# Position-bias products of two chunks put two steps away from the attention's scores, and the left half of the bias tile read backwards from PSUM

## Chip, core and metric

The kernel runs on one core of a Trainium2 chip. The metric is device time in microseconds (us) of one execution. Five engines matter: TensorE (PE in the profile; PEld is its weight load), VectorE (DVE), ScalarE (ACT), GpSimd (POOL) and SyncE (SP). The last two issue most of the DMAs.

## What is computed

The reference runs attention with a position bias, then two feed-forward layers, on 4 batches, 8 heads, 576 positions and 64 features a head:

```python
scores = scale * np.matmul(q, k.transpose(0, 1, 3, 2))
x = (psi_rel / psi_i)[..., None]      # log1p|i-j| / log1p(max(i,1))
bias = np.maximum(x @ w1 + b1, 0.0) @ w2   # hidden 32, one value per head
attn = softmax(scores + bias) ;  attn_out = attn @ v
x = (sigmoid(x @ w_gate) * (x @ w_val)) @ w_out      # 512 -> 1536 -> 512
h = x @ w_in ;  out = (h * clip(h + 3, 0, 6) / 6) @ w_out2   # 512 -> 2048 -> 512
```

## The kernel before, in words

The 576 query positions are cut into five chunks (`QC`: 128, 128, 128, 128 and 64 rows, numbered 0 to 4). The attention of chunk 0 runs alone in a **lead**. Then come five **blocks**: block k runs the two feed-forward layers for the tokens of chunk k, 68 **steps** of twelve matmuls each (`product`, L554; kinds G and V, then Y, H and O, H, O), and between its steps stands the attention of chunk k+1. `block_events` makes a list of events, each with a due time counted in steps, and `block` runs an event ahead of the first step whose number is not below its due time. TensorE's order is just this order of writing. Beginning with block 1, the orders of ScalarE, VectorE and the DMA queues are chosen by a scheduler when the kernel is built; in block 0 it chooses ScalarE's and VectorE's.

The **bias of a chunk** is made one chunk ahead, in groups G of 16 rows. `bias_hidden` writes the hidden layer into tiles z (two calls on ScalarE, L147, two on VectorE, L149; two buffers). `bias_mm` multiplies by w2 (L160 in chunks 1 to 3, L168 in chunks 0 and 4). Chunks 1 to 3 are **mirrored**: only distances 0, 1, 2, ... are computed, once for each row, and `bias_out2` spreads two groups over a tile bo with rows of SU = 607 values: distances to the right in order, by ScalarE (L182), distances to the left in reverse order, by VectorE (L185). Two DMAs (L192) take bo to memory, from where `bias_read` fetches it as bm. `chunk_bias(c, t0, dt)` makes the events: z of group g at t0 + dt g, the products of groups g and g+1 at t0 + dt g + dt + 1.

The **attention of chunks 2 to 4** goes in pairs of (head pair, batch) units. For pair p `pair_qk` forms the scores (L426 in chunks 2 and 3): first the last 256 columns of both units, into two tiles of the pool `ps_m`, then the first 320 columns, one unit after the other, into two tiles of the pool `ps_s`. VectorE adds the bias and takes the minimum (L448), ScalarE takes exponentials (L314), VectorE normalises (L327) and transposes (L353), DMAs turn the result, and `pair_av` (L384) multiplies by the values, two pairs later.

The pool `ps_s` has two buffers in PSUM, taken in turn, and serves both the bias products and the 320-column scores:

```python
s1 = pool("ps_s", 2, space=PS)
m1 = pool("ps_m", 4, space=PS)
```

In block 1 the pairs stand at due times 21 + d i with d = (67 - 21)/9 = 5.11, and the products of chunk 3's bias at 31.21, 36.32, 41.43 and 46.54, each 0.01 of a step ahead of a pair. So TensorE meets, ahead of one step: `pair_av` of an old pair, the bias products, `pair_qk`. In block 2 d is 8.14, and the two products of chunk 4's bias come ahead of the pairs due at 16.79 and 33.07 in the same way.

Of the kernel before, what the change touches and what calls it, by code (L numbers as in the profile page):

```python
# [9 lines left out]
F32 = mybir.dt.float32  # L10
F32R = mybir.dt.float32r
U32 = mybir.dt.uint32
AF = mybir.ActivationFunctionType
ALU = mybir.AluOpType
AX = mybir.AxisListType

B, H, S, D = 4, 8, 576, 64
# [13 lines left out]
SU = S + 31  # L31
# [27 lines left out]
def fused_kernel(ctx: ExitStack, tc: tile.TileContext, qd, kd, vd, tz, td, rd, zc, w2b, iden, wpack, out):  # L59
    nc = tc.nc  # L60
# [21 lines left out]
    def mm_ps():  # L82
        return m1.tile([128, 512], F32, name="ps")
# [11 lines left out]
    cv_t = const.tile([128, 1], F32, name="cv_t")  # L95
# [11 lines left out]
    ps = mm_ps()  # L107
# [6 lines left out]
    ps = mm_ps()  # L114
    for g in (2, 3):
        nc.tensor.matmul(
            out=ps[32 * g:32 * g + 32, 0:2], lhsT=w2b_t, rhs=zc_t[:, 0:2], start=True, stop=True,
# [7 lines left out]
    A, z_q, bo_q = {}, {}, {}  # L125

    def mirrored(G):
        return QC[1][0] <= 16 * G < QC[NC - 1][0]

    def reach(G):  # L130

        i0 = 16 * (G & ~1)
        left, right = i0 + 31, S - 1 - i0
        return left, right, max(left, right) + 1

    def bias_hidden(G, g):

        if g == 0:
            z_q[G] = z_p.tile([128, 4, S], F32, name="z")
        t = 4 * G + g  # L140
        if mirrored(G):
            n = reach(G)[2]
            z, x = z_q[G][:, g, 0:n], td_t[:, 0:n]
        else:
            z, x = z_q[G][:, g], tz_t[:, S - 4 - 4 * t:2 * S - 4 - 4 * t]
        if g < 2:
            nc.scalar.activation(out=z, in_=x, func=AF.Relu, scale=sc_t[:, t:t + 1], bias=b1c)  # L147
        else:
            nc.vector.tensor_scalar(  # L149
                out=z, in0=x, scalar1=sc_t[:, t:t + 1], scalar2=zc_t[:, 2:3], op0=ALU.mult, op1=ALU.max  # L150
            )

    def bias_mm(G):
        z = z_q.pop(G)
        if mirrored(G):
            if G % 2 == 0:
                bo_q[G] = s_ps()
            ps, n = bo_q[G & ~1], reach(G)[2]
            for g in range(4):
                nc.tensor.matmul(  # L160
                    out=ps[32 * g:32 * g + 32, G % 2, 0:n], lhsT=w2b_t, rhs=z[:, g, 0:n],
                    start=True, stop=True, tile_position=(0, 32 * g),
                )
            return
        ps = bo_q[G] = s_ps()
        for j in range(2):
            for g in range(4):
                nc.tensor.matmul(  # L168
                    out=ps[32 * g:32 * g + 32, j, 0:NI], lhsT=w2b_t, rhs=z[:, g, NI * j:NI * j + NI],
                    start=True, stop=True, tile_position=(0, 32 * g),  # L170
                )

    bo_t = {}

    def bias_out2(G):

        ps = bo_q.pop(G)
        c = 16 * G // NQ
        i0 = 16 * G - QC[c][0]
        left, right, _ = reach(G)  # L180
        bo = A["bo"].tile([128, 2, SU], F32, name="bo")
        nc.scalar.activation(  # L182
            out=bo[:, :, left:], in_=ps[:, :, 0:right + 1], func=AF.Identity, scale=D ** 0.5, bias=cv_t
        )
        nc.vector.tensor_scalar(  # L185
            out=bo[:, :, left - 1::-1], in0=ps[:, :, 1:left + 1],
            scalar1=D ** 0.5, scalar2=cv_t, op0=ALU.mult, op1=ALU.add,
        )
        at = NQ - 32 - i0
        rows = biasD[c].rearrange("(h r w) -> r h w", h=H, w=SW)[i0:i0 + 32, :, at:at + SU]  # L190
        for x in range(2):
            nc.sync.dma_start(  # L192
                out=rows[16 * x:16 * x + 16], in_=bo[:, x],
            )

    def bias_out(G, x=0, last=True):

        ps = bo_q.pop(G)
        c = min(G // 8, NC - 1)
        if x == 0:  # L200
            bo_t[0] = A["bo"].tile([128, 2, SU], F32, name="bo")[:, :, 0:S]
        bo = bo_t[0][:, x]
        bv = bo.rearrange("p (a j) -> p a j", a=2)
        if c:
            nc.scalar.activation(out=bv, in_=ps[:, :, 0:NI], func=AF.Identity, scale=D ** 0.5, bias=cv_t)
        else:
            nc.vector.tensor_scalar(
                out=bv, in0=ps[:, :, 0:NI], scalar1=D ** 0.5, scalar2=cv_t, op0=ALU.mult, op1=ALU.add
            )
        i0 = 16 * G - QC[c][0]  # L210
        if c == 0:
            for h in range(2):
                nc.sync.dma_start(out=bm_q[0, 0][i0:i0 + 16, h], in_=bo.rearrange("(i h) j -> h i j", h=H)[h])
        if last:
            (nc.gpsimd if c == 0 else nc.sync).dma_start(
                out=biasD[c][i0 - 16 * x:i0 + 16].rearrange("(g i) h j -> (i h) g j", i=16),
                in_=bo_t[0][:, 0:x + 1],
            )
# [406 lines left out]
    with ExitStack() as lead:  # L625
# [11 lines left out]
        for G in range(NG0 + NG1 + 1):  # L637
            if G == NG0:
                bias_out(G - 1, (G - 1) % 2, G % 2 == 0)
            if G < NG0 + NG1:  # L640
                for g in range(4):
                    bias_hidden(G, g)
                bias_mm(G)
            if G and G < NG0:
                bias_out(G - 1, (G - 1) % 2, G % 2 == 0)
            if G == NG0 + NG1:
                bias_out2(NG0)
# [45 lines left out]
    def chunk_bias(c, t0, dt, done=0):  # L693

        i0, n = QC[c]
        G0, nG = i0 // 16 + done, n // 16 - done
        ev = []
        for g in range(nG):
            ev.append((t0 + dt * g, lambda G=G0 + g: [bias_hidden(G, t) for t in range(4)]))
        for g in range(0, nG, 2):  # L700
            def outs(G=G0 + g, two=min(2, nG - g)):
                for i in range(two):
                    bias_mm(G + i)
                if mirrored(G):
                    bias_out2(G)
                    return
                for i in range(two):
                    bias_out(G + i, i, i == two - 1)
            ev.append((t0 + dt * g + dt + 1, outs))
        return ev  # L710

    def chunk_att(c, t0, t1, lag):

        us = units[c]
        d = (t1 - t0) / (len(us) - 1 + lag)
        ev = [
            (t0 - 2 * d, lambda: att_load(us[0], False)),
            (t0 - d, lambda: (bias_read(us[0]), load_rows(us[1]), load_k(us[1]))),
        ]
        for i, u in enumerate(us):  # L720
            a = t0 + d * i

            def first(u=u, nxt=us[i + 2] if i + 2 < len(us) else None):
                if nxt:
                    load_rows(nxt)
                    load_k(nxt)
                att_qk(u)
                att_min(u)
                att_exp(u)
                att_norm(u)  # L730
            if i:
                ev.append((a + 0.5, lambda u=u: load_v(u)))
            for part in range(3):
                ev.append((a + lag * d - 3 + part, lambda u=u, p=part: att_tr(u, p, mm_ps)))
            ev.append((a + lag * d - 0.01, lambda u=u: (att_av(u, mm_ps), att_x(u))))
            ev.append((a, first))
        return ev
# [45 lines left out]
    def block_events(k):  # L783
        ev = []
        last = NSTEP - 1
        if k == 0:
            ev.append((1.0, lambda: nc.sync.dma_start(out=td_t[:, t0:], in_=td[:, t0:])))
            ev += chunk_bias(1, 2.0, 1.5, NG1)
            ev += chunk_att(1, 15.5, last, 2)
        elif k == 1:  # L790
            d = (last - 21.0) / 9
            ev += chunk_bias(2, 2.0, 1.5)
            ev += chunk_pairs(2, 21.0, d, 2 * d, last)
            ev += chunk_bias(3, 19.99 + 1.5 * d, d / 2)
        elif k == 2:
            d = (last - 9.5 - 0.5) / 7
            n4 = 2 * S - 4 - 4 * 16 * 8
            ev.append((0.1, lambda: nc.sync.dma_start(out=tz_t[:, 0:n4], in_=tz[:, 0:n4])))
            ev += chunk_pairs(3, 0.5, d, d, last)
            ev += chunk_bias(4, d - 0.51, d)  # L800
        elif k == 3:
            ev += chunk_pairs(4, 0.5, (last - 10.5) / 3, 10.0, last)
        return [e[::2] for e in sorted((e[0], n, e[1]) for n, e in enumerate(ev))]
# [90 lines left out]
```

## Time and profile before

| | |
|---|---|
| Time of the kernel before, median of 3 runs | 1126.38 us (1126.29 to 1127.05) |
| The profiled execution: its own time | 1126.06 us |
| The profiled execution: span of its instructions | 1124.3 us |
| TensorE busy | 1099.5 us, 98% of the span |
| VectorE, ScalarE, GpSimd busy | 670.3, 525.5, 126.1 us |

The span runs from the first to the last instruction; the execution's own time has 1.76 us more around it. Busy time is not the same as progress: an engine's share is an average over stages, and what a wait costs is read from the stage in which it stands.

### The profile page before, as it was taken

To read this page: it belongs to the slowest core of one execution; us is meant where nothing else is said; L and a number is where in the kernel's file an instruction comes from. 1 tells how busy PE (TensorE), PEld (TensorE's weight loads), DVE (VectorE), ACT (ScalarE), POOL (GpSimd) and SP (SyncE) were. 2 spreads that over 40 slices of the span, in tenths; PEclk is the share of its full clock that TensorE was granted. 3 is DMA by queue.
4 is the path that set the end of the run, shared out by engine and by line. 5 is a ranking of instruction groups with operands and counts; after the bars stand their busy time and mean duration, and the time that the engine had idled before them with its cause. 6 is when DMAs were issued, how large, how long until landed. Compare 5 with 4: busy or idle time off the path is not lost.

```text
span 1124.3 us, 19865 instructions
## 1 busy us (share of the span) xinstructions
PE 1099.5 (98%) x7142; PEld 887.0 (79%) x7142; DVE 670.3 (60%) x1529; ACT 525.5 (47%) x1050; POOL 126.1 (11%) x240
## 2 busy tenths in 40 slices
PE   6899999999999999999999999999999999999998
PEld 3577677777778778677888878788878787879998
DVE  5698998989892446797735564656452507052232
ACT  5587877788882542564513342444222205131231
POOL 0000000000001001211221111111340202031000
PEclk9899999999999999999999999999999999999999
DMA  4875999999987778899898878888897977768997
GB/s 161 289 250 196 329 399 382 387 348 333 414 319 266 214 248 288 269 305 294 280 343 256 281 248 276 257 259 266 257 297 244 255 255 242 238 214 298 366 364 271
DMA packets 119281, 321.97 MB, mean 286 GB/s; under 512 B 21008, under 2 KB 29712, under 8 KB 119184
## 3 DMA queue, kind: packets, MB, share of 16 engines
q1 hardware_dynamic: 109152, 299.63, 78.0%
q0 software_dynamic: 8512, 20.72, 6.7%
q8 instruction: 57, 0.93, 0.3%
q10 hardware_dynamic: 1520, 0.35, 0.1%
q14 instruction: 40, 0.33, 0.1%
HBM read 245.09 MB, written 51.37 MB: 264 GB/s over the span
## 4 chain that ended last, share of the span: by engine, by line
PE 90%; DVE 4%; DMA 3%; ACT 1%; issue 1%; SPq 0%; DVEq 0%; ACTq 0%
PE ps L554 72%; PE ps L384 7%; PE ps L289 3%; PE ps L340 3%; PE ps L426 2%; PE ps L160 1%; DVE z L149 1%; DMA bm<-bo 1%; DMA kt<-kd 1%; PE ps L432 1%; DMA wp<-wsp 1%; DMA biasD<-bo 0%; DVE bo L185 0%; ACT z L147 0%; DMA vt<-vd 0%
## 5 line engine op out<-in xcount | busy, mean ns | idle before, releaser
L554 PE MATMUL ps<-xyh,wp 128*128 128x512 f32 (+1 forms) x1600 | 467.2, 372 | 2.2 <-DVE wp L535 1.4
L554 PEld LDWEIGHTS ps<-xyh,wp 128*128 128x128 f32 x1600 | 290.2, 189 | 62.2 <-issue 4.4
L554 PE MATMUL ps<-gh,wp 128*128 128x512 f32 (+1 forms) x1120 | 329.7, 372 | 0.1
L554 PE MATMUL ps<-xyl,wp 128*128 128x512 f32 (+1 forms) x800 | 295.3, 369 | 0.3 <-DVE xyl L567 0.3
L554 PEld LDWEIGHTS ps<-gh,wp 128*128 128x128 f32 x1120 | 203.4, 189 | 36.7 <-issue 2.0
L554 PE MATMUL ps<-gl,wp 128*128 128x512 f32 (+1 forms) x560 | 206.5, 369 | 0.0
L554 PEld LDWEIGHTS ps<-xyl,wp 128*128 128x128 f32 x800 | 150.9, 189 | 24.7 <-DVE xyl L567 0.8
L363 POOL DMA_DIRECT2D pT<-t x192 | 94.6, 499 | 504.5 <-DVE t L353 161.4
L563 ACT ACTIVATE gh<-tmp 128x512 fp32r<-128x512 f32 (+1 forms) x140 | 82.2, 588 | 143.7 <-DVE tmp L585 105.4
L314 ACT ACTIVATE s<-s,m 128x576 f32<-128x576 f32 x144 | 110.4, 769 | 22.3 <-DVE m L448 15.4
L554 PEld LDWEIGHTS ps<-gl,wp 128*128 128x128 f32 x560 | 105.7, 189 | 16.7 <-DVE gl L565 0.5
L565 DVE TENSOR_TENSOR gl<-tmp,gh 128x512 fp32r<-128x512 f32 (+1 forms) x140 | 88.5, 634 | 46.0 <-ACT gh L563 45.2
L585 DVE SCALAR_TENSOR_TENSOR tmp<-tmp,ps 128x512 f32<-128x512 f32 (+1 forms) x60 | 37.9, 631 | 93.2 <-PE ps L554 93.1
L384 PEld LDWEIGHTS ps<-pT,vt 128*64 128x64 f32 x1600 | 79.0, 137 | 16.2 <-issue 13.4
L384 PE MATMUL ps<-pT,vt 128*64 128x128 f32 (+1 forms) x1600 | 91.3, 266 | 0.1
L591 DVE SCALAR_TENSOR_TENSOR tmp<-tmp,ps 128x512 f32<-128x512 f32 (+1 forms) x80 | 50.1, 629 | 55.0 <-ACT tmp L590 53.4
L615 POOL DMA_DIRECT2D outT<-acc x40 | 28.1, 744 | 366.5 <-DVE r L322 302.3
L404 ACT ACTIVATE xyh<-ps 128x128 fp32r<-128x128 f32 (+1 forms) x52 | 16.5, 318 | 109.6 <-PE ps L384 109.4
L405 DVE TENSOR_TENSOR xyl<-ps,xyh 128x128 fp32r<-128x128 f32 (+1 forms) x52 | 17.7, 341 | 80.5 <-ACT xyh L404 80.4
L590 ACT ACTIVATE tmp<-ps 128x512 f32<-128x512 f32 (+1 forms) x80 | 44.0, 550 | 45.1 <-PE ps L554 44.2
L581 ACT ACTIVATE tmp<-ps 128x512 f32<-128x512 f32 (+1 forms) x60 | 33.2, 553 | 59.9 <-PE ps L554 59.9
L147 ACT ACTIVATE z<-tz_t,zc_t,sc_t 128x576 f32<-128x576 f32 (+7 forms) x72 | 51.0, 763 | 19.4 <-PE ps L160 10.2
(69 smaller groups left out, 1101.6 us busy)
## 6 DMA issues: line engine op xcount, KB each, us to landing
wp<-wsp SPq DMA_DIRECT2D x272, 512.0 KB, 5.2
wd<-wpack SPq DMA_DIRECT2D x68, 512.0 KB, 6.7
wsp<-wp SPq DMA_DIRECT2D x68, 512.0 KB, 6.1
vt<-vd SPq DMA_DIRECT2D x80, 320.0 KB, 5.0
kt<-kd SPq DMA_DIRECT2D x80, 288.0 KB, 5.0
pT<-t POOLq DMA_DIRECT2D x192, 72.0 KB, 4.7
pT<-t SPq DMA_DIRECT2D x128, 72.0 KB, 4.4
bm<-biasD SPq DMA_DIRECT2D x15, 576.0 KB, 5.6
```

Of the source, the lines that this page charges most:

```text
L147: nc.scalar.activation(out=z, in_=x, func=AF.Relu, scale=sc_t[:, t:t + 1], bias=b1c)
L289: nc.tensor.matmul(out=ps[h][n * a:n * a + n, j, 0:NI], lhsT=qt[r, b + a, 0:n], rhs=kt[r, NI * j:NI * j + NI], start=True, stop=True, tile ...
L314: nc.scalar.activation(out=s[:, h], in_=s[:, h], func=AF.Exp, scale=-1.0, bias=d["m"][:, h:h + 1], accum_out=r[:, h:h + 1],)
L340: nc.tensor.transpose(out=ps[:, t * NQ:t * NQ + NQ], in_=p[:, 128 * k:128 * k + 128], identity=id_t)
L363: (nc.sync if p[0][0] < 4 and i > 1 else nc.gpsimd).dma_start(out=pt[32 * q:32 * q + 32, i].rearrange("j u t i -> j (u t i)"), in_=t[32 * ...
L384: nc.tensor.matmul(out=po[64 * h:64 * h + 64, n * a:n * a + n], lhsT=vt[:, v], rhs=pt[:, m * a:m * a + m, k, :], start=(t == 0), stop=(t = ...
L554: nc.tensor.matmul(out=ps[:, 0:nt], lhsT=w[:, c, :], rhs=x[:, 0:nt], start=(first and c == 0 and i == 0), stop=(last and c == 3 and i == 2),)
L563: nc.scalar.activation(out=hi[:, 0:nt], in_=src, func=AF.Copy, scale=scale)
L565: nc.vector.tensor_tensor(out=lo[:, 0:nt], in0=src, in1=hi[:, 0:nt].bitcast(F32), op=ALU.subtract)
L585: nc.vector.scalar_tensor_tensor(out=th, in0=th, scalar=1.0, in1=ps, op0=ALU.add, op1=ALU.mult)
L590: nc.scalar.activation(out=t, in_=ps, func=AF.Relu, bias=3.0)
L591: nc.vector.scalar_tensor_tensor(out=t, in0=t, scalar=6.0, in1=ps, op0=ALU.min, op1=ALU.mult)
```

## The change

Four edits. The tile bo gets rows of 608 values, of which 607 are used. The left half of a mirrored tile is no longer written backwards but read backwards from PSUM and written forwards. For chunk 1 (made in the lead and in block 0) ScalarE does that as well as the right half; for chunks 2 and 3 VectorE still does. And the due times of the bias of chunk 3 (in block 1) and of chunk 4 (in block 2) are put 3.21 steps later.

```diff
-        bo = A["bo"].tile([128, 2, SU], F32, name="bo")
+        bo = A["bo"].tile([128, 2, SU + 1], F32, name="bo")
         nc.scalar.activation(
-            out=bo[:, :, left:], in_=ps[:, :, 0:right + 1], func=AF.Identity, scale=D ** 0.5, bias=cv_t
+            out=bo[:, :, left:SU], in_=ps[:, :, 0:right + 1], func=AF.Identity, scale=D ** 0.5, bias=cv_t
         )
-        nc.vector.tensor_scalar(
-            out=bo[:, :, left - 1::-1], in0=ps[:, :, 1:left + 1],
-            scalar1=D ** 0.5, scalar2=cv_t, op0=ALU.mult, op1=ALU.add,
-        )
+        if c == 1:
+            nc.scalar.activation(
+                out=bo[:, :, 0:left], in_=ps[:, :, left:0:-1], func=AF.Identity, scale=D ** 0.5, bias=cv_t
+            )
+        else:
+            nc.vector.tensor_scalar(
+                out=bo[:, :, 0:left], in0=ps[:, :, left:0:-1],
+                scalar1=D ** 0.5, scalar2=cv_t, op0=ALU.mult, op1=ALU.add,
+            )
...
-                out=rows[16 * x:16 * x + 16], in_=bo[:, x],
+                out=rows[16 * x:16 * x + 16], in_=bo[:, x, 0:SU],
...
-            bo_t[0] = A["bo"].tile([128, 2, SU], F32, name="bo")[:, :, 0:S]
+            bo_t[0] = A["bo"].tile([128, 2, SU + 1], F32, name="bo")[:, :, 0:S]
...
-            ev += chunk_bias(3, 19.99 + 1.5 * d, d / 2)
+            ev += chunk_bias(3, 23.2 + 1.5 * d, d / 2)
...
-            ev += chunk_bias(4, d - 0.51, d)
+            ev += chunk_bias(4, d + 2.7, d)
```

With the new due times the four products of block 1 fall at 34.42, 39.53, 44.64 and 49.75, three steps behind one pair and two steps ahead of the next; those of block 2 at 19.99 and 36.27. In the changed kernel every line below L198 has a number higher by 5: L554 is L559, L426 is L431, L384 is L389, L448 is L453, L353 is L358, L314 is L319.

TensorE in block 1, at the first bias product of chunk 3, before (gh and gl are the halves of the gated activations, wp the weights, pT the turned attention, kh and qh the high halves of keys and queries):

```order
L554 MATMUL ps<-gh,wp 128x512
L384 MATMUL ps<-pT,vt 64x128 x20
L160 MATMUL ps<-z,w2b_t 32x416 x8
L426 MATMUL ps<-kh,qh 128x256 x2
L426 MATMUL ps<-kh,ql 128x256 x2
L426 MATMUL ps<-kl,qh 128x256 x2
```

And the same product in the changed kernel, where 36 matmuls of the feed-forward layers (three steps) stand between the scores and it, and 24 (two steps) between it and the next values product:

```order
L559 MATMUL ps<-gh,wp 128x512 x2
L559 MATMUL ps<-gl,wp 128x512
L559 MATMUL ps<-gh,wp 128x512
L160 MATMUL ps<-z,w2b_t 32x416 x8
L559 MATMUL ps<-gh,wp 128x512
L559 MATMUL ps<-gl,wp 128x512
```

The bias product has moved from between the values product and the scores to a place between two feed-forward steps; nothing else on TensorE in this block has changed its neighbours.

VectorE at the second bias product of chunk 3 in block 1, before (the transposes of the pair before it stand a few rows further up):

```order
L591 SCALAR_TENSOR_TENSOR tmp<-tmp,ps 128x512
L565 TENSOR_TENSOR gl<-tmp,gh 128x512
L405 TENSOR_TENSOR xyl<-ps,xyh 128x256
L149 TENSOR_SCALAR z<-tz_t,sc_t,zc_t 128x480 x4
L185 TENSOR_SCALAR bo<-ps,cv_t 128x2x447
L448 ISA s,m<-ps,bm 128x256
L448 ISA m 128x1
```

And in the changed kernel, where z and bo of the same groups stand on the other side of the next pair's minimum, among its normalising and transposes:

```order
L596 SCALAR_TENSOR_TENSOR tmp<-tmp,ps 128x512
L149 TENSOR_SCALAR z<-tz_t,sc_t,zc_t 128x480 x4
L358 STREAM_TRANSPOSE t<-s 128x4x288 x2
L570 TENSOR_TENSOR gl<-tmp,gh 128x512
L190 TENSOR_SCALAR bo<-ps,cv_t 128x2x447
L596 SCALAR_TENSOR_TENSOR tmp<-tmp,ps 128x512 x2
L570 TENSOR_TENSOR gl<-tmp,gh 128x512 x2
L410 TENSOR_TENSOR xyl<-ps,xyh 128x256
L453 ISA s,m<-ps,bm 128x256
```

VectorE's z and bo no longer stand directly ahead of the next pair's minimum (L453); the feed-forward's tmp and gl of the steps that follow the bias product now stand behind them.

ScalarE in block 0, at the third bias tile of chunk 1, before (cm and wp are stages of the weights' unpacking):

```order
L147 ACTIVATE z<-tz_t,zc_t,sc_t 128x352 x2
L563 ACTIVATE gh<-tmp 128x512
L182 ACTIVATE bo<-ps,cv_t 128x2x384
L147 ACTIVATE z<-tz_t,zc_t,sc_t 128x352 x2
L524 ACTIVATE cm<-wd 128x512
L534 ACTIVATE wp<-cm 128x512
```

And in the changed kernel:

```order
L568 ACTIVATE gh<-tmp 128x512
L147 ACTIVATE z<-tz_t,zc_t,sc_t 128x352
L182 ACTIVATE bo<-ps,cv_t 128x2x384
L186 ACTIVATE bo<-ps,cv_t 128x2x223
L147 ACTIVATE z<-tz_t,zc_t,sc_t 128x352 x2
L529 ACTIVATE cm<-wd 128x512
L539 ACTIVATE wp<-cm 128x512
```

One more instruction, the left half, stands ahead of the next weights on ScalarE; on VectorE its L185 is gone.

## Rows read from the trace of the kernel before

**Rows 1.** The page's first part: busy us of each engine, share, instructions.

```profile
PE 1099.5 (98%) x7142; PEld 887.0 (79%) x7142; DVE 670.3 (60%) x1529; ACT 525.5 (47%) x1050; POOL 126.1 (11%) x240
```

**Rows 2.** Stretches of block 0 and block 1: us, busy time of each engine.

```profile
96.00:168.00 72.00, 70.16 (x355) 51.76 (x351) 67.61 (x131) 54.64 (x96) 0.00 (x0) 1.00 0.92 340
...
350.00:520.00 170.00, 165.52 (x1007) 128.44 (x1007) 107.07 (x245) 80.58 (x148) 21.16 (x42) 1.00 0.83 264
```

**Rows 3.** The waits of TensorE's matmuls: total us, times, longest us.

```profile
PE ps L426 <- DVE bo L185: 4.5, 4, 1.2
...
PE ps L554 <- DVE wp L535: 1.4, 2, 0.8
...
PE ps L289 <- DVE bo L185: 1.0, 1, 1.0
PE ps L426 <- ACT bo L205: 0.7, 1, 0.7
PE ps L554 <- ACT wp L534: 0.7, 1, 0.7
```

**Rows 4.** The chain that ended last, in block 1: start us, us, what.

```profile
365.68 1.21 PE ps L160 x16
...
375.32 1.21 PE ps L160 x16
...
449.37 2.33 PE ps L384 x40
451.70 1.53 PE ps L160 x16
...
456.37 13.84 PE ps L554 x60
...
477.38 13.82 PE ps L554 x60
...
512.27 2.33 PE ps L384 x40
...
519.68 13.82 PE ps L554 x60
...
535.84 1.79 PE ps L426 x24
```

**Rows 5.** The timeline at chunk 3's first bias product (idle before, releaser, in brackets).

```profile
453.93 0.56 ACT L182 ACTIVATE bo<-ps,cv_t 128x384 f32<-128x384 f32 x1
...
454.53 1.08 DVE L185 TENSOR_SCALAR bo<-ps,cv_t 128x830 f32<-128x830 f32 x1
...
455.67 0.42 PE L426 MATMUL ps<-kh,qh 64*128 64x320 f32 x2 [1.08 <-DVE bo L185]
```

**Rows 6.** The timeline at chunk 4's first bias product, in block 2.

```profile
646.07 2.15 PE L168 MATMUL ps<-z,w2b_t 128*32 128x288 f32 x32
...
650.89 0.50 PE L554 MATMUL ps<-xyh,wp 128*128 128x512 f32 x1
```

**Rows 7.** Groups by form, of the bias tile's halves: count, busy us, mean ns.

```profile
L185 DVE TENSOR_SCALAR bo<-ps,cv_t 128x1022 f32<-128x1022 f32 x1 | 1.3, 1283 | 0.0
...
L182 ACT ACTIVATE bo<-ps,cv_t 128x896 f32<-128x896 f32 x1 | 1.0, 1009 | 4.5 <-PE ps L160 4.5
...
L185 DVE TENSOR_SCALAR bo<-ps,cv_t 128x382 f32<-128x382 f32 x1 | 0.6, 614 | 0.0
L182 ACT ACTIVATE bo<-ps,cv_t 128x384 f32<-128x384 f32 x1 | 0.6, 561 | 0.0
```

**Rows 8.** VectorE's timeline around chunk 3's second bias product.

```profile
473.50 2.04 DVE L149 TENSOR_SCALAR z<-tz_t,sc_t,zc_t 128x480 f32<-128x480 f32 x4
475.47 1.15 DVE L185 TENSOR_SCALAR bo<-ps,cv_t 128x894 f32<-128x894 f32 x1
...
487.46 0.69 DVE L565 TENSOR_TENSOR gl<-tmp,gh 128x512 fp32r<-128x512 f32 x1
488.06 1.37 DVE L353 STREAM_TRANSPOSE t<-s 128x1152 f32<-128x1152 f32 x1
```

## The prediction

> **What bounds the kernel now.** I read the page's first part first: TensorE is busy for 98% of the span, VectorE for 60%, ScalarE for 47% [rows 1]. The reader should see two things there. No edit that shortens another engine's work is worth its own duration, and all that can be won without taking matmuls away is TensorE's idle time, 1124.3 - 1099.5 = 24.8 us. The second view is busy time by stretch, which says where that idle time lies [rows 2]. Block 0 between 96 and 168 us has 1.84 us of it, with VectorE busy for 67.6 of 72 us; the stretch from 350 to 520 us, nearly all of it block 1, has 4.48. (Most of the rest lies in the lead, ahead of 96 us, and at the very end, where the change does almost nothing.)
>
> The third view, the waits of TensorE's matmuls, gives the names [rows 3]. The largest in block 1 is L426, a pair's scores, waiting for VectorE's L185, the left half of a bias tile: 4.5 us in four waits of at most 1.2. The same scores wait 0.7 us for ScalarE's L205, chunk 4's bias. In block 0 the feed-forward matmul L554 waits 1.4 us for VectorE and 0.7 for ScalarE, both on unpacked weights.
>
> The fourth view shows one of the four. The bias product takes one of the two `ps_s` buffers, and the scores that follow need both. ScalarE's right half starts at 453.93, VectorE's left half runs from 454.53 for 1.08 us, and only then does the second unit's score matmul start, after 1.08 us of idleness [rows 5]. VectorE here is not overloaded; the matmul was issued while the buffer was still being emptied. The wait is thus a matter of place.
>
> **The bias products of chunk 3 (block 1).** What does one meeting cost? From the end of the values product to the first feed-forward matmul the chain gives 456.37 - (449.37 + 2.33) = 4.67 us at the first, and 519.68 - (512.27 + 2.33) = 5.08 at the last of four [rows 4]; their mean, 4.88, makes 19.5 for four. The scores alone take 1.79 [rows 4], so the bias costs 19.5 - 4 x 1.79 = 12.3 us as it stands.
>
> What does it cost between two feed-forward steps, where the change puts it? The trace has that case in the same block, for chunk 2. From one bias product to the next are 375.32 - 365.68 = 9.64 us, with three steps (36 matmuls) between; 60 matmuls take 13.84, so 36 take 8.30, and the product costs 1.34 with its changeovers, of which 1.21 is its own [rows 4]. That one is 320 columns wide. The one of 416 columns takes 1.53 [rows 4], 0.32 more for 96 columns, so the four of 416 to 512 cost 1.66 to 1.98, together 7.3. The saving is 12.3 - 7.3 = **5.0 us**; at least the 4.5 us of waits should go, unless new ones come.
>
> Would new ones come? Ahead of the product: z has been ready since the buffer came free one period earlier, and its `ps_s` buffer was freed by the pair's minimum, which runs within a few us of the scores; three steps are 8.3 us. Behind it: the buffer has to be empty when the next pair's second unit starts, and bo stands now behind the two transposes in VectorE's order. At the second product the later transpose ended at 488.06 + 1.37 = 489.43, which is 12.1 us after those scores ended at 477.38 [rows 4, 8]. Put the four z (2.04), one gl (0.69) and bo (1.15) on top, and bo ends 15.9 us after the scores [rows 8]. The next pair's second unit starts after five steps (13.82), a bias product of 1.8, the values of 2.33 and half of 1.79 [rows 4], together 18.9 us. The margin is 3.0 us. A second one: the step right behind the product keeps its `ps_m` buffer until VectorE's tmp has read it, and tmp, one operation of gl's size, now stands behind bo, so by 16.6 us. With four buffers taken in turn (two steps, the values, two column tails) that buffer is wanted by the second tail at 13.82 + 1.8 + 2.33 = 18.0. The margin is 1.4 us. I count no new wait, and keep up to 2 us for it.
>
> **The bias products of chunk 4 (block 2).** At the first, from the product's start to the feed-forward are 650.89 - 646.07 = 4.82 us; less the product's 2.15, which it needs anywhere, and 1.79 for the scores, 0.88 is left [rows 4, 6]. Of it 0.7 is the wait on L205 [rows 3]. I take **0.9**; the second product stands ahead of the values product, whose 2.33 us cover the emptying, and shows no wait: 0.
>
> **The left half of chunk 1 on ScalarE.** The trace of before shows no backward read from PSUM. A row of 382 elements took VectorE 614 ns, one of 384 on ScalarE, read forwards, 561 [rows 7]; the slopes are (1283 - 614)/640 = 1.05 ns an element on VectorE and (1009 - 561)/512 = 0.88 on ScalarE. VectorE's rows are the nearest to the unknown: they ran backwards on the writing side. If backward costs nothing, the three tiles in block 0 (382, 446, 510 elements) take 614 + 681 + 748 = 2.04 us from VectorE and give ScalarE 0.56 + 0.62 + 0.67 = 1.85. If a backward read ran at half the rate, ScalarE would get 1.2 us more, and VectorE's reads for chunks 2 and 3 would grow by up to 1.1 us each, inside the 3.0 us of margin. I take no penalty.
>
> In block 0 VectorE has no room and ScalarE has 72 - 54.64 = 17.4 us of it in that stretch [rows 2]. The weights pass through both engines in turn, so relief of the fuller one should shorten the 1.4 + 0.7 = 2.1 us that L554 waits for them [rows 3]. But ScalarE's two halves now stand in one piece of some 1.4 us ahead of its next weight, and both orders were drawn up anew. Bounds: a gain of 2.1 (all those waits), a loss of 1.85 (all of ScalarE's new work shows). I take half of the gain, **1.0**.
>
> The Trainium skill, "ScalarE: Activation LUTs", section Rules for kernel authors, speaks against this edit: additions and multiplications belong on VectorE, which it says is up to about three times as fast per element in bf16. The rows of this kernel, fp32 out of PSUM, have ScalarE the faster by 9% [rows 7]. By the rule at its fullest, and if nothing hid it, ScalarE would need 3 x 2.04 = 6.1 us for the three tiles (an estimate from that page), and the sum below would come to 1126.5 instead.
>
> In the lead the first scores wait 1.0 us for L185 [rows 3]. ScalarE would do both halves one after the other, and one hand-over between engines falls away; the 318 elements cost about 0.51 instead of 0.55. I take 0.1 there.
>
> **Rows of 608.** The second row of the tile starts 4 bytes further on; nothing waits for the tile's DMAs on the path, since the bias is wanted a block later. Cost 0, and it would only show if SP's queue, which issues the weights behind these DMAs, stood still for more than the five steps by which weights are loaded ahead, 13.8 us.
>
> **Sum.** 5.0 + 0.9 + 1.0 + 0.1 = 7.0 us off 1126.06, the profiled execution's own time (1124.3 of span and 1.76 around it): 1119.1. The median of the runs shown is 0.3 higher, so I predict 1119.4, 0.62% less than 1126.38.
>
> **Rivals.** (a) *The waits go, but VectorE's crowd after a pair makes smaller ones.* For it: z and bo, 3.2 us, now join the 12.1 us of work that follow the scores, and margins of 1.4 and 3.0 us are worked out from one period. Against it: VectorE is busy for only 107 of 170 us [rows 2]. Say 1 us at three of the four products: 1122.4. (b) *Block 0 loses.* ScalarE's piece delays weights for which TensorE waits already; instead of 1.0 gained, 1.85 lost: 1122.2. (c) *Slower than before.* The place is the second and third product of block 1. If bo ends so late that the next pair's second unit waits longer than it did (1.1 to 1.2 us), the meeting has only been moved, and tmp and gl behind bo are held up with it. To cost more than the 7.0 us won, VectorE must come 3.0 + 7.0/3, about 5.3 us, later than worked out at each of three products; that gives 1126.4 and more. (d) *No effect*: the waits on L185 stay because something else keeps the buffer, for example the right half on ScalarE behind its queue. Then only block 0's and the lead's 1.1 us come: 1125.3. ScalarE's busy share there (80.6 of 170 us) speaks against it.
>
> **How the numbers follow.** My forecast has 0.72; its own range is 1117.9 (all waits of block 0 gone) to 1121. Rival (a) has 0.12, (b) 0.09, (c) 0.03, (d) 0.04. The range that is to hold 8 in 10 reaches over (a) and (b), each with a little more than its price (0.7), and down to the case in which all 2.1 us of block 0 and all of the lead's 1.0 are won: 1117.3 to 1123.0. A measurement of this kernel can tell some 0.2%, 2.3 us, from no change. Faster than 1124.1 are the forecast, (a) and (b), 0.92 with a little off for (a) being worse than said; within 0.2% lies (d) and the tail of (a), 0.05; slower 0.03.
>
> **What would show it right or wrong.** In the profile after, the waits of L431 on bo (L190 and L210) are gone, and the stretch 350 to 520 has under 1 us of TensorE idle. From values to feed-forward matmul a pair takes 2.33 + 1.79 in all eight cases, and a bias product between steps costs 1.7 to 2.0. Block 0's waits on weights fall to about 1 us. The step L186 has rows of about 0.51 to 0.67 us; if they are twice as long, backward reading is dear. The prediction is wrong if L559 in blocks 1 or 2 waits for tmp, xyl or gl, or L431 for bo again, for more than 2 us together, or if block 0 idles over 2 us longer.

## The result, and the profile after

| | before | after |
|---|---|---|
| median of five runs each, side by side | 1127.05 us (1126.29 to 1128.65) | 1114.02 us (1111.63 to 1116.05) |
| ratio after / before, 95% interval | | 0.9884 [0.9867, 0.9902] |
| profiled execution: own time, span | 1126.06, 1124.3 us | 1114.02, 1112.2 us |

The change is worth 13.0 us, 1.16%. The forecast was 1119.4 with a range of 1117.3 to 1123.0: the sign was right, the size was not, and the time lies below the range. The kernel gained nearly twice what was worked out.

Where did 12.1 us of span come from? Five places that both programs pass, from the two timelines and chains (us from the start):

| place | before | after | gained so far |
|---|---|---|---|
| first scores of the lead | 32.48 | 22.77 | 9.71 |
| first feed-forward matmul (block 0 begins) | 97.01 | 85.20 | 11.81 |
| a run of 70 feed-forward matmuls at the start of block 1 | 349.56 | 341.37 | 8.19 |
| fifth values product of block 1's pairs | 533.50 | 520.98 | 12.52 |
| end of the span | 1124.3 | 1112.2 | 12.1 |

The lines of the first four places, before (two of the timeline, two of the chain):

```profile
32.48 0.75 PE L289 MATMUL ps<-kt,qt 64*128 64x288 f32 x2
...
97.01 0.50 PE L554 MATMUL ps<-xyh,wp 128*128 128x512 f32 x1
...
349.56 16.11 PE ps L554 x70
...
533.50 2.33 PE ps L384 x40
```

and after (the fifth values product stands further down):

```profile
22.77 0.75 PE L294 MATMUL ps<-kt,qt 64*128 64x288 f32 x2
...
85.20 0.50 PE L559 MATMUL ps<-xyh,wp 128*128 128x512 f32 x1
...
341.37 16.11 PE ps L559 x70
```

So the lead gave 11.8 us where 0.1 was forecast, block 0 took back 3.6 where a gain of 1.0 was forecast, and block 1 gave 4.3 of a forecast 5.0. Behind block 1 another 0.75 is gained in block 2 (below) and 1.2 is lost elsewhere, the largest piece a pause of 0.71 us at 838 us for which the profile names no cause. (The two profiled executions lie 12.0 us apart and the medians 13.0, because the profiled execution of the kernel before was 1.0 us faster than its median.)

TensorE's busy time is what it was [rows 1]; the span around it has shrunk:

```profile
PE 1098.6 (99%) x7142; PEld 885.2 (80%) x7142; DVE 667.9 (60%) x1525; ACT 526.9 (47%) x1054; POOL 126.4 (11%) x240
```

Busy time by stretch, after (us, then busy time of TensorE, its weight load, VectorE, ScalarE, GpSimd, then the granted clock, the DMA share, GB/s). The first two rows answer to [rows 2]:

```profile
96.00:168.00 72.00, 68.39 (x341) 49.80 (x340) 64.09 (x125) 52.52 (x96) 0.00 (x0) 0.98 0.96 353
350.00:520.00 170.00, 170.00 (x1027) 131.92 (x1026) 111.95 (x263) 83.81 (x156) 19.69 (x40) 1.00 0.82 263
...
147.00:153.00 6.00, 4.99 (x19) 3.53 (x18) 5.48 (x10) 3.72 (x7) 0.00 (x0) 0.72 1.02 404
```

Block 1's stretch has no idle time left (170.00 of 170). Block 0's has more than it had (72 - 68.39 = 3.61 us against 1.84), and for six microseconds of it the granted clock is 0.72 (0.51 from 149 to 152 us, so the lower of its two levels, 1.2 and 2.4 GHz).

The waits of TensorE's matmuls, after, to be laid beside [rows 3] (total us, times, longest):

```profile
PE ps L559 <- ACT wp L539: 2.6, 2, 1.3
...
PE ps L559 <- DVE wp L540: 1.0, 1, 1.0
PE ps L294 <- ACT bo L186: 0.8, 1, 0.8
...
PE ps L559 <- DVE xyl L572: 0.3, 1, 0.3
PE ps L559 <- DVE gl L570: 0.3, 1, 0.3
```

The scores of pairs no longer wait for a bias tile at all; what the weights cost in block 0 went up from 2.1 to 3.6 us. Block 1 in the chain, after (start us, us, what), which answers to [rows 4]:

```profile
441.18 2.33 PE ps L389 x40
443.51 1.79 PE ps L431 x22
445.30 8.37 PE ps L559 x36
453.67 1.53 PE ps L160 x16
455.20 5.71 PE ps L559 x24
460.91 2.33 PE ps L389 x40
...
513.42 1.85 PE ps L160 x16
515.27 5.71 PE ps L559 x24
520.98 2.33 PE ps L389 x40
```

Values, scores, three steps, the bias product, two steps, values: the meeting is gone, and from values to feed-forward matmul are 2.33 + 1.79 (at the fourth product 2.33 + 2.00).

**The lead.** TensorE's waits name VectorE's L207 for less than half of 10 us there (4.6). VectorE's own show all of it. The waits of all engines in the first 40 us, before:

```profile
DVE bo L207 <- DMA bm<-bo: 10.0, 4, 3.3
...
PE ps L168 <- DVE bo L207: 4.6, 2, 3.0
```

And VectorE's timeline, before, at the third and fourth rows of chunk 0's tiles (the bracket is the idle time before, and what ended it):

```profile
13.05 0.81 DVE L207 TENSOR_SCALAR bo<-ps,cv_t 128x576 f32<-128x576 f32 x1
13.78 1.06 DVE L149 TENSOR_SCALAR z<-tz_t,sc_t,zc_t 128x576 f32<-128x576 f32 x2
18.11 0.82 DVE L207 TENSOR_SCALAR bo<-ps,cv_t 128x576 f32<-128x576 f32 x1 [3.27 <-DMA bm<-bo]
```

The same two in the changed kernel:

```profile
11.11 0.81 DVE L212 TENSOR_SCALAR bo<-ps,cv_t 128x576 f32<-128x576 f32 x1
11.84 1.06 DVE L149 TENSOR_SCALAR z<-tz_t,sc_t,zc_t 128x576 f32<-128x576 f32 x2
12.82 0.81 DVE L212 TENSOR_SCALAR bo<-ps,cv_t 128x576 f32<-128x576 f32 x1
```

A tile of chunk 0 holds two groups, one in each row, and `bias_out` writes them with two instructions. Each row is read by two DMAs of its own (bm<-bo) as soon as it is there. In the kernel before, the instruction that writes the second row waits until the DMAs that read the first have landed, four times, though the rows share no element. This is not a choice of the chip: the wait is a semaphore condition that is put on the instruction when the kernel is built, and with 608 values a row it is not in the program. (The change's line with `bo_t[0]`, in `bias_out`, is where this tile is made.) The edit "Rows of 608", which the prediction put at nothing, is thus the first suspect for nearly the whole surplus.

### The profile page after: what moved, and what is told of

It is laid out like the page before. It is cut to its first block, busy times and chain, and to the rows that moved or that the text cites. A ratio compares the mean times of both kernels' runs of the same rounds, so it can differ in the third digit from the quotient of the medians.

```text
span 1112.2 us, 19855 instructions
## 1 busy us (share of the span) xinstructions
PE 1098.6 (99%) x7142; PEld 885.2 (80%) x7142; DVE 667.9 (60%) x1525; ACT 526.9 (47%) x1054; POOL 126.4 (11%) x240
## 4 chain that ended last, share of the span: by engine, by line
PE 94%; DVE 3%; DMA 1%; ACT 1%; issue 1%; SPq 0%; ACTq 0%; DVEq 0%
PE ps L559 73%; PE ps L389 8%; PE ps L294 3%; PE ps L345 3%; PE ps L431 2%; PE ps L160 2%; PE ps L168 1%; PE ps L437 1%; DMA wd<-wpack 1%; DVE s L453 1%; ACT z L147 1%; DMA bm<-biasD 0%; DVE s L332 0%; DMA sc_t<-rd 0%; DVE kl L275 0%
## 5 line engine op out<-in xcount | busy, mean ns | idle before, releaser
L559 PE MATMUL ps<-xyh,wp 128*128 128x512 f32 (+1 forms) x1600 | 469.8, 373 | 3.8 <-ACT wp L539 2.6
L559 PEld LDWEIGHTS ps<-xyh,wp 128*128 128x128 f32 x1600 | 290.8, 189 | 66.9 <-issue 6.9
L559 PE MATMUL ps<-gh,wp 128*128 128x512 f32 (+1 forms) x1120 | 330.0, 372 | 0.0
L559 PE MATMUL ps<-xyl,wp 128*128 128x512 f32 (+1 forms) x800 | 296.0, 370 | 0.3 <-DVE xyl L572 0.3
L559 PEld LDWEIGHTS ps<-gh,wp 128*128 128x128 f32 x1120 | 203.4, 189 | 37.9 <-issue 2.7
L559 PE MATMUL ps<-gl,wp 128*128 128x512 f32 (+1 forms) x560 | 206.5, 369 | 0.3 <-DVE gl L570 0.3
L559 PEld LDWEIGHTS ps<-xyl,wp 128*128 128x128 f32 x800 | 151.3, 189 | 24.7 <-DVE xyl L572 0.8
L319 ACT ACTIVATE s<-s,m 128x576 f32<-128x576 f32 x144 | 110.5, 769 | 24.8 <-DVE m L453 14.9
L559 PEld LDWEIGHTS ps<-gl,wp 128*128 128x128 f32 x560 | 105.7, 189 | 17.0 <-DVE gl L570 0.9
L389 PEld LDWEIGHTS ps<-pT,vt 128*64 128x64 f32 x1600 | 79.1, 137 | 16.9 <-issue 14.1
L389 PE MATMUL ps<-pT,vt 128*64 128x128 f32 (+1 forms) x1600 | 91.5, 266 | 0.8 <-issue 0.7
L147 ACT ACTIVATE z<-tz_t,zc_t,sc_t 128x576 f32<-128x576 f32 (+7 forms) x72 | 51.2, 765 | 14.5 <-PE ps L160 12.1
```

Of the source, the lines that this page charges most:

```text
L319: nc.scalar.activation(out=s[:, h], in_=s[:, h], func=AF.Exp, scale=-1.0, bias=d["m"][:, h:h + 1], accum_out=r[:, h:h + 1],)
L389: nc.tensor.matmul(out=po[64 * h:64 * h + 64, n * a:n * a + n], lhsT=vt[:, v], rhs=pt[:, m * a:m * a + m, k, :], start=(t == 0), stop=(t = ...
L559: nc.tensor.matmul(out=ps[:, 0:nt], lhsT=w[:, c, :], rhs=x[:, 0:nt], start=(first and c == 0 and i == 0), stop=(last and c == 3 and i == 2),)
```

## The experiments

The kernel before ran again beside each group of runs: 1127.64 us beside the four runs of "Each part alone", 1127.79 beside rows of 610, chunk 0 alone, and one and two tiles, 1128.33 beside rows of 614 and 612 and the lead alone. Between groups the ratios compare better than the times.

Theories after the result: (T1) the width of the rows takes away the false wait, about 12 us; (T2) ScalarE's left half costs block 0 the 3.6 us; (T3) the moved bias products give 4.3 + 0.75. Rivals: the prediction's (width nothing, ScalarE a gain), and that block 0 loses because the lead is shorter.

### Each part alone

**Width only.** The kernel before, with

```diff
-        bo = A["bo"].tile([128, 2, SU], F32, name="bo")
+        bo = A["bo"].tile([128, 2, SU + 1], F32, name="bo")
```

at both places, and :SU where the tile is written and sent.

> The kernel before with only the rows of 608; the left half still comes from VectorE in every block, the bias products of later chunks stand where they stood. Theory (with rows of 607 the second row of a chunk-0 tile waits for the DMAs that read the first row, 10.0 us in four waits, and with 608 it does not): the first scores start at about 24.4 us instead of 34.2, TensorE's granted clock behind them is higher, the first feed-forward matmul stands near 88.8 instead of 100.6, and if the rest of the kernel keeps its pace the time is about 1127.0 - 11.8 = 1115.2. If a shorter lead costs block 0 the 3.6 us that it lost in the changed kernel, it is 1118.8. Rival, as the prediction had it (the width costs and gives nothing; the lead is shorter because ScalarE makes the left half): 1127, and the wait of L207 for the DMAs that read the tile is still 10 us.

Measured: 1117.37 us (1116.03 to 1118.39), ratio to the kernel before 0.9905 [0.9888, 0.9921], so 10.3 us from one number, between the expectation's 1115.2 and 1118.8. First scores at 22.71, first feed-forward matmul at 86.62; no wait of L207 for a DMA. (The expectation's 24.4 and 88.8 are later marks than those of the table above, the second unit's scores and the first feed-forward matmul that waits; here these stand at 24.46 and 90.21.) T1 holds, the rival falls. From the first feed-forward matmul to the run of 70 in block 1 it needs 254.27 us, between the 252.55 of before and the 256.17 of after.

**Everything but the width.** The changed kernel, with

```diff
-        bo = A["bo"].tile([128, 2, SU + 1], F32, name="bo")
+        bo = A["bo"].tile([128, 2, SU], F32, name="bo")
```

at both places.

> The changed kernel with rows of 607 again, all else as changed. Theory: the waits of L212 for the DMAs that read the tile come back (about 10 us in four), the first feed-forward matmul stands near 100.6 again, and the time is 1114.0 + 11.8 = 1125.8 if block 0 loses its 3.6 us in any case, or about 1122.2 if it lost them only because the lead was shorter. Rival (the width does nothing): 1114, within 1 us.

Measured: 1126.23 us (1123.38 to 1131.91), ratio 0.999 [0.9976, 1.0004]. Without the padding the change as a whole can't be told from nothing. VectorE's waits in the first 40 us:

```profile
DVE bo L212 <- DMA bm<-bo: 10.0, 4, 3.3
```

Block 0 takes 257.00 us here, with a late lead: it does not lose because the lead is shorter. (The profiled execution is the longest of the twelve, with one wait of 4.5 us on gl at 574 us, behind transposes of VectorE that wait for a DMA; the others' times don't suggest it.)

**VectorE makes the left halves again.** The changed kernel, with

```diff
-        if c == 1:
+        if c == 9:
             nc.scalar.activation(
```

so that the branch to ScalarE is never taken.

> The changed kernel with the left half of chunk 1 on VectorE (read backwards from PSUM, as for the later chunks), all else as changed. Theory (block 0 loses 3.6 us because the ScalarE instructions added there put the unpacking of a weight behind the softmax, after which TensorE idles 1.3 + 1.0 us near 145 us and runs the next 5 us at a granted clock of about 0.7): that place has no such wait and no fall of the clock, and the time is 1114.0 - 3.6 = 1110.4. Rival A (block 0 loses because the lead is shorter and the weights come late whoever makes the left half): 1114, within 1 us. Rival B, the prediction's own (ScalarE's help in block 0 is worth 1.0 us, 0.1 in the lead): 1115.1.

Measured: 1110.53 us (1109.91 to 1111.90), ratio to before 0.9848 [0.983, 0.9867]: 3.5 us less than the changed kernel, as T2 says. The granted clock is 1.00 between 84 and 168 us, and block 0 up to the run of 70 takes 253.93 us, 2.2 less than in the changed kernel. This version beats both kernels.

**The two due times alone.** The kernel before, with

```diff
-            ev += chunk_bias(3, 19.99 + 1.5 * d, d / 2)
+            ev += chunk_bias(3, 23.2 + 1.5 * d, d / 2)
...
-            ev += chunk_bias(4, d - 0.51, d)
+            ev += chunk_bias(4, d + 2.7, d)
```

> The kernel before with only the two changed due times: the bias products of chunk 3 and chunk 4 between feed-forward steps, rows of 607, left halves by VectorE, written backwards. Prediction's sum for these two terms: 5.0 + 0.9 = 5.9 us, so 1127.0 - 5.9 = 1121.1. From the changed kernel's trace: 4.3 in block 1 and 0.75 in block 2, so 1122.0. Rival (part of what block 1 won came from the width or from reading backwards, so that bo is earlier empty): under 3 us, 1124 or more. Lead and block 0 are as in the kernel before.

Measured: 1123.37 us (1121.35 to 1128.05), ratio 0.9963 [0.995, 0.9977], 4.3 us. In its trace, block 1 from the run of 70 to the fifth values product takes 529.48 - 350.10 = 179.38 us, against 183.94 before: 4.56. The move needs neither the width nor the backward read. T3 holds; the time shows a little less than the prediction's 5.9, which lies just outside the interval (2.6 to 5.6 us).

### Which widths, and which tile

In the programs as built, the wait stands at second rows when a row has 607, 609, 610, 611 or 614 values, and not with 608, 612 or 616. Three widths and one mixed kernel were run, all with VectorE's left halves; the edit is the number behind SU.

**Rows of 610.**

```diff
-        bo = A["bo"].tile([128, 2, SU + 1], F32, name="bo")
+        bo = A["bo"].tile([128, 2, SU + 3], F32, name="bo")
```

> The kernel of the run with VectorE's left halves (1110.5), with rows of 610 in place of 608: longer still, but not a multiple of four elements. Theory (what matters is whether the second row of a tile begins on a multiple of four elements, 16 bytes; in the program as built its first instruction waits for the first row's DMAs with 607, 609, 610, 611 and 614 and not with 608, 612 and 616): the waits of L212 for the DMAs that read the tile are back, about 10 us in four, the first scores stand near 34 us, and the time is 1110.5 + 11.8, about 1122.3. Rival (any gap behind the first row would do): 1110.5, no such wait.

Measured: 1129.36 us (1128.34 to 1132.22), ratio to before 1.0015 [1.0006, 1.0025]. A longer row is not enough, so the rival falls: VectorE waits for bm<-bo again (8.2 us in three waits that are put down to it). But the kernel is 7 us worse than T1 allows. The trace shows where: matmuls that read gh and gl are longer (396 and 394 ns by the median, instead of 389).

**Rows of 614 and of 612** (SU + 7, SU + 5), to part the two causes.

> The kernel of the run with VectorE's left halves (1110.5), with rows of 614. Like 610 this is not a multiple of four elements, so the waits for the tile's DMAs are in the program; unlike 610 it moves the tiles that lie behind the bias tiles in SBUF by a multiple of 64 bytes (with 610 the tiles gh and gl are moved by 32, and their matmuls took 396 and 394 ns by the median instead of 389). Theory of two causes (the waits cost about 12 us, the moved tiles the rest of what the run with 610 lost): the waits of L212 are about 10 us, the matmuls of gh take 389 ns, and the time is 1110.5 + 11.8 = 1122.3. Rival (one cause: all that 610 lost hangs on the waits or on the row's length): 1129, as with 610.

> The kernel of the run with VectorE's left halves (1110.5), with rows of 612: a multiple of four elements, so no wait for the tile's DMAs, but the tiles gh and gl lie 32 bytes further on, as with 610. Theory of two causes: no waits of L212 for DMAs, the first scores near 23 us, the matmuls of gh and gl at about 395 ns, and the time is 1110.5 plus the rest of what 610 lost (1129.4 - 1122.3 = 7.1), so 1117.6. Rival (where the tiles lie does nothing; the longer matmuls came from the lead being late): 1110.5 with 389 ns.

Measured: 614 gives 1124.04 us (1123.04 to 1125.75), ratio 0.9967 [0.9954, 0.9981], with 10.2 us of waits in four; 612 gives 1117.26 us (1116.62 to 1117.81), ratio 0.9902 [0.9887, 0.9918], without them and with first scores at 22.77. Matmuls of the feed-forward layers between 820 and 1010 us (duration ns min/median/max, first and last start), with 608:

```profile
L559 PE MATMUL ps<-gh,wp x224: 388/389/497, 875.2 to 1007.9; 128*128 128x512 f32 x112
...
L559 PE MATMUL ps<-gl,wp x112: 388/389/395, 875.4 to 1007.7; 128*128 128x512 f32 x112
```

with 612:

```profile
L559 PE MATMUL ps<-gh,wp x216: 393/396/505, 878.8 to 1007.9; 128*128 128x512 f32 x108
...
L559 PE MATMUL ps<-gl,wp x108: 392/394/397, 879.1 to 1007.6; 128*128 128x512 f32 x108
```

and with 614:

```profile
L559 PE MATMUL ps<-gh,wp x203: 392/394/501, 886.6 to 1009.7; 128*128 128x512 f32 x102
...
L559 PE MATMUL ps<-gl,wp x102: 388/388/398, 886.8 to 1010.0; 128*128 128x512 f32 x102
```

Two causes, as expected: the waits (614: 1124.04 - 1110.53 = 13.5 us, of which gh's and gl's matmuls are 0.8) and the moved tiles (612: 6.7 us, or 6.1 by the ratios; gh's and gl's matmuls are busy for 4.9 us more, 541.9 against 537.0). The other tiles that lie behind bo move along, so where the remaining 1 to 2 us come from is open. One detail of the expectation missed: with 614 gh's matmuls took 394 ns, not 389, though gl's did not grow.

**Only chunk 0's tiles padded** (607 in `bias_out2`, 608 in `bias_out`).

```diff
-        bo = A["bo"].tile([128, 2, SU + 1], F32, name="bo")
+        bo = A["bo"].tile([128, 2, SU], F32, name="bo")
...
             bo_t[0] = A["bo"].tile([128, 2, SU + 1], F32, name="bo")[:, :, 0:S]
```

> The kernel of the run with VectorE's left halves (1110.5), with rows of 608 for chunk 0's tiles alone (L206) and 607 for the mirrored tiles of later chunks (L181). Theory (the four waits all stand at L212, second rows of chunk 0's tiles; the mirrored tiles write both rows with one instruction and can't wait for each other): 1110.5, within 1 us. Rival (the width also changes what the DMAs of the mirrored tiles cost or when they land): more than 1.5 us slower than 1110.5.

Measured: 1112.05 us (1110.57 to 1113.84), ratio 0.9859 [0.9841, 0.9876]; first scores at 22.73. It is 1.5 us over the run with all tiles padded, just more than the expected 1 us and no more than the rival's 1.5; the two intervals overlap, and of the profiled executions this one is the shorter (1110.57 against 1111.90). The gain sits in the lead's tiles, and a small share for the mirrored ones is not excluded.

### What costs block 0 its 3.6 us

In the changed kernel TensorE stands still twice at the first pair of block 0:

```profile
144.60 0.39 PE L559 MATMUL ps<-xyh,wp 128*128 128x512 f32 x1
146.33 0.50 PE L559 MATMUL ps<-xyh,wp 128*128 128x512 f32 x1 [1.34 <-ACT wp L539]
146.67 0.39 PE L559 MATMUL ps<-xyl,wp 128*128 128x512 f32 x1
148.07 0.85 PE L559 MATMUL ps<-xyh,wp 128*128 128x512 f32 x2 [1.01 <-DVE wp L540]
...
149.14 1.06 PE L559 MATMUL ps<-xyh,wp 128*128 128x512 f32 x2
```

Behind the waits two matmuls take 1.06 us instead of 0.62; ten of them run from 148.07 to 152.14, 1.8 us more than at 0.23 each. Waits and clock are 2.35 + 1.8 = 4.1 us; the kernel before waits 0.5 us a little further on (at 168.39), where the changed one does not, which leaves 3.6. That the sum comes out so exactly is in part chance: block 0 of the kernel before is among the shortest of all (252.55 us), and against the run with VectorE's left halves (253.93) the changed kernel loses 2.2. ScalarE at that place:

```profile
143.10 0.78 ACT L319 ACTIVATE s<-s,m 128x576 f32<-128x576 f32 x1 [2.19 <-DVE m L309]
...
144.35 0.76 ACT L319 ACTIVATE s<-s,m 128x576 f32<-128x576 f32 x1
...
145.11 0.64 ACT L529 ACTIVATE cm<-wd 128x512 f32<-128x512 f32 x1
145.66 0.62 ACT L539 ACTIVATE wp<-cm 128x512 fp32r<-128x512 f32 x1
```

The weight that TensorE wants stands behind both softmax instructions, and these wait 2.19 us for VectorE's minimum. In the kernel before an unpacking step stood ahead of them:

```profile
153.66 0.63 ACT L534 ACTIVATE wp<-cm 128x512 fp32r<-128x512 f32 x1 [2.11 <-DVE cm L529]
...
154.68 0.77 ACT L314 ACTIVATE s<-s,m 128x576 f32<-128x576 f32 x1
```

ScalarE's left halves lie some 20 us further up, the last at 124.0. So is it their work, or the order that was drawn up anew because of them? Two kernels tell it apart, because the orders come out the other way round from the work: with one left half on ScalarE the order is the bad one, with two it is the good one.

```diff
-        if c == 1:
+        if c == 1 and left in (223,):
```

> The changed kernel with ScalarE making the left half of one tile of block 0 only, that of 446 elements (about 0.62 us of ScalarE); VectorE makes the others. ScalarE's order behind the last bias tile is here word for word that of the changed kernel: the second unpacking step stands behind both softmax instructions. Order theory (block 0 loses because of that order, not because of the work): TensorE waits for ScalarE's unpacked weight again near 145 us, 1.3 us and 1.0 for VectorE behind it, the granted clock falls behind it, and the time is about 1114.0. Work theory (ScalarE's added time is what shows, a third of the 3.5 us for a third of the 1.85 us): 1111.7, and no fall of the clock.

```diff
-        if c == 1:
+        if c == 1 and left in (223, 255):
```

> The changed kernel with ScalarE making the left halves of two tiles of block 0, those of 446 and 510 elements (about 1.29 us of ScalarE), VectorE the others. ScalarE's order behind the last tile is here that of the kernel before: an unpacking step stands ahead of the softmax. Order theory: more work for ScalarE than in the run with one tile, and yet about 1110.5, with waits for weights of under 2 us in block 0 and no fall of the clock near 150 us. Work theory: two thirds of the 3.5 us, so 1112.9, slower than the run with one tile.

Measured: one tile 1114.75 us (1114.15 to 1117.51), ratio 0.989 [0.9874, 0.9906]; two tiles 1110.71 us (1110.56 to 1114.07), ratio 0.9856 [0.9836, 0.9876]. TensorE with one tile:

```profile
146.56 0.50 PE L559 MATMUL ps<-xyh,wp 128*128 128x512 f32 x1 [1.33 <-ACT wp L539]
148.30 0.73 PE L559 MATMUL ps<-xyh,wp 128*128 128x512 f32 x2 [1.01 <-DVE wp L540]
```

ScalarE with two tiles:

```profile
142.45 0.64 ACT L539 ACTIVATE wp<-cm 128x512 fp32r<-128x512 f32 x1 [2.11 <-DVE cm L534]
142.99 0.58 ACT L586 ACTIVATE tmp<-ps 128x512 f32<-128x512 f32 x1
143.46 0.77 ACT L319 ACTIVATE s<-s,m 128x576 f32<-128x576 f32 x1
```

The waits of 1.3 and 1.0 us come back to the place with a third of the work, and are absent with two thirds of it. It is the order. (ScalarE's and VectorE's orders were drawn up together and both differ, so the runs do not say which of the two does it. Right behind the last left half TensorE waits 1.24 us at 126 us after, 1.25 with two tiles; the kernel before waits 0.66 + 0.84 there, so the work itself costs nothing at that place.) The three kernels with that order (after, rows of 607, one tile) need 256.17, 257.00 and 255.82 us from the first feed-forward matmul to the run of 70; before and the nine others lie between 252.50 and 254.73. What was expected and did not come: in the profiled execution with one tile the granted clock stayed at 1.00 behind the same two waits, so the 1.8 us of clock belong to some executions. That execution, of 1117.27 us, is 2.5 us over the median of its kernel and shows waits of 2.9 us on gl and 1.6 on a DMA behind 550 us, which have no part in block 0.

**ScalarE in the lead alone** (`c == 1 and left < 191`, so the tile of 318 elements).

> The changed kernel with ScalarE making the left half of the lead's tile alone (318 elements) and VectorE those of block 0's three; ScalarE's order in block 0 is that of the run with VectorE's left halves. Prediction's term for the lead: 0.1 less, so 1110.4; the scores' wait on the tile goes from 1.0 us to about 0.8. Rival (this part of the change is also redrawn into a loss): 1112 or more.

Measured: 1111.40 us (1110.93 to 1113.21), ratio 0.9856 [0.9837, 0.9875]. The first scores' wait is 0.8 instead of 1.0 us, as expected, but the first feed-forward matmul stands at 85.80, against 85.56 with VectorE. Neither the gain of 0.1 nor a loss can be told from these runs.

## Why the prediction was wrong, step by step

- **Rows of 608: cost 0. This step failed.** It argued that "nothing waits for the tile's DMAs on the path, since the bias is wanted a block later". That is true of the mirrored tiles; the padded line in `bias_out` makes chunk 0's tiles, which the lead needs at once. The 10.0 us stood in the profile of before, but among VectorE's waits, and the prediction used TensorE's alone [rows 3]; and of the 24.8 us of TensorE's idle time the part ahead of 96 us was set aside as a place "where the change does almost nothing". The runs put this edit at 12.2 us (after against 607), 10.3 (alone) and 13.5 (608 against 614). That the sign came out right is therefore luck: with rows of 607 the rest of the change, from which 7.0 us were worked out, comes to a ratio of 0.999 [0.9976, 1.0004], since what the moved products gain ScalarE's left halves lose again.
- **The lead: 0.1.** It came to 11.8, of which 9.7 are there at the first scores. The other 2.1 come between these and the feed-forward. In the 22 us behind the first scores the granted clock was 0.92, against 0.77 before, but the run with VectorE's left halves had 1.00 and began block 0 no earlier (85.56); so the clock explains them only in part, and the rest is open.
- **Chunk 1's left half on ScalarE: a gain of 1.0, bounds 2.1 and -1.85.** It lost 3.5 (against VectorE's left halves) and 2.9 (rows of 607, against the moves alone), both outside the bounds by the medians, though the single runs spread by as much; in the profiled executions block 0 is 2.2 us longer than with VectorE's left halves. The prediction's own sign, block 0 idle for over 2 us longer, did not quite come (3.61 against 1.84 us), because part of the loss was clock. Durations were right: 382 elements took 567 ns forecast at 0.56 us, and backward reading is free on both engines (below). The text named the danger, "both orders were drawn up anew", and gave it no price: the bound of 1.85 was ScalarE's work, while the loss was an unpacking step put behind two others, which the work doesn't bound. Rival (b) had this sign, with 0.09. The rule cited from the Trainium skill ("ScalarE: Activation LUTs", Rules for kernel authors) speaks against the edit because of ScalarE's rate in bf16; the rows after, in fp32, do not show that (567 ns against VectorE's 614, [rows 7]), and the loss has another cause.
- **Block 1: 5.0.** Right in mechanism: 4.3 after, 4.56 alone. The waits on bo are gone, the 3.0 and 1.4 us of margin held (waits on gl and xyl of 0.3 each). Mis-sized was the product between steps: from values to values, less 2.33 for the values, 13.83 for 60 matmuls and the scores, there are 1.78, 1.89, 2.00 and 2.12 us, together 7.8 where 7.3 was worked out. The fourth scores took 0.2 longer, and 12.3 - 7.8 - 0.2 is the 4.3 that was measured.
- **Block 2: 0.9.** The time gained so far grows from 12.13 us (588.25 before, 576.12 after) to 12.88 (677.10, 664.22) over the first meeting: 0.75. The wait on L205 is gone; right.

ScalarE's and VectorE's left halves by form, after (count, busy us, mean ns), beside [rows 7]:

```profile
L186 ACT ACTIVATE bo<-ps,cv_t 128x446 f32<-128x446 f32 x1 | 0.6, 612 | 0.0
L186 ACT ACTIVATE bo<-ps,cv_t 128x382 f32<-128x382 f32 x1 | 0.6, 567 | 0.0
...
L190 DVE TENSOR_SCALAR bo<-ps,cv_t 128x1022 f32<-128x1022 f32 x1 | 1.3, 1274 | 0.0
```

Read backwards, 1022 elements take VectorE 1274 ns; written backwards they took 1283.

## What to carry to other kernels

When a diff touches a tile's shape, look at every place that makes that tile, and in the waits of all engines (not TensorE's alone) for an instruction that waits for a DMA of a part which it does not touch; such a wait can hang on nothing but the length of a row. Idle time in a part of the program which a change does not seem to concern is to be explained before it is set aside. And an edit that only hands an engine a little work can cost more than that work where a scheduler draws the order anew: price the place on the path where the order differs, not the instruction.

## What was not expected of the hardware

- **Where a tile lies changes how long matmuls that read it take.** With rows of 612 or 610 the tiles gh and gl lie 32 bytes further on in SBUF, and 512-column matmuls on them take 396 and 394 ns by the median instead of 389; the matmuls on xyh, which did not move, stayed at 389. With 64 bytes (614) gh's took 394 and gl's 388. The kernel with rows of 612 is 6.7 us slower than with 608, 4.9 of it in these matmuls. Which property of the place decides is open.
- **The granted clock can fall behind a short wait, and need not.** After 1.34 and 1.01 us of idleness it was 0.72 over the six microseconds from 147 us in the changed kernel, a stretch at 1.2 GHz among such at 2.4, and the same 0.72 from 160 us with rows of 607; with one tile on ScalarE, after 1.33 and 1.01 us, it was 1.00.
